# Attention scores with K as the moving operand in two of eight head pairs, and a second exponent in place of a copy of p, in a two-layer decode kernel

## The chip, the core and the metric

The kernel runs on one NeuronCore of a Trainium2 chip. Five engines have their own instruction streams: TensorE (PE in the profile, its weight loads PEld), VectorE (DVE), ScalarE (ACT), GpSimd (POOL) and SyncE (SP), which here only issues DMAs. The time is that of the device for one execution, in microseconds (us); the kernel before was run three times: 1097.86, 1098.34 and 1098.76 us, median 1098.34.

## The reference

Eight sequences (B = 8), one new token each, width D = 448. Two layers run one after the other, each an attention over a cache of 4096 keys followed by a small MLP block; both layers use the same caches and weights.

```python
def _A_ref(x, k_cache, v_cache, wq, wo):
    B, Sq, D = x.shape
    Hq, Dh = 16, 256
    Hkv = k_cache.shape[1]          # 8
    rep = Hq // Hkv                 # 2
    q = (x @ wq).reshape(B, Sq, Hq, Dh).transpose(0, 2, 1, 3)
    k = jnp.repeat(k_cache, rep, axis=1)
    v = jnp.repeat(v_cache, rep, axis=1)
    scores = jnp.einsum("bhqd,bhkd->bhqk", q, k) * (Dh ** -0.5)
    p = _softmax(scores, axis=-1)
    o = jnp.einsum("bhqk,bhkd->bhqd", p, v)
    return o.transpose(0, 2, 1, 3).reshape(B, Sq, Hq * Dh) @ wo
...
x = A_x
x = x + _A_ref(_layernorm(x), A_k_cache, A_v_cache, A_wq, A_wo)
x = x + _B_ref(_layernorm(x), B_w1, B_w2, B_w3, B_w4)
x = x + _A_ref(_layernorm(x), A_k_cache, A_v_cache, A_wq, A_wo)
x = x + _B_ref(_layernorm(x), B_w1, B_w2, B_w3, B_w4)
```

Each of the two caches holds 8 x 8 x 4096 x 256 bf16, 134 MB. Two query heads share one head of K and V.

## The kernel before

**Pieces and slots.** A head's K or V is read as four pieces of 128 partitions x 2048 bf16 (0.52 MB); each piece holds 1024 keys, 8 to a partition. Pieces lie in 31 equal slots of SBUF. Two heads make a pair m, four pairs (m = 0 to 3) a sequence. One DMA brings one, two or four neighbouring pieces (0.5, 1 or 2 MB) into neighbouring slots.

**What runs over what.** For each sequence b the first layer's four pairs are done, then the MLP and the new queries, then the second layer's four pairs, mixed with the first layer's pairs of sequence b + 1. K of pairs 1, 2 and 3 (24 pieces) stays in its slots from the first layer to the second, so only pair 0's K is read twice; V is read in both layers. The stretch from the end of a sequence's first layer to its first scores in the second, about 22 us, is called its turn (`turn`): a chain of small steps on TensorE, VectorE and ScalarE (MLP, query projection), during which the V of the previous sequence's second-layer pairs 2 and 3 streams through the few slots that are left.

**Scores** (`kpart`). K has to be turned so that the key's features lie on partitions. This is done in one of two ways. With `NN` a pair says how many pieces of each head TensorE transposes (line 810, into PSUM; ScalarE copies them back, line 871); these are scored by line 881 (K stationary, two columns of queries). All other pieces are transposed in 32 x 32 blocks by VectorE, half a piece to an instruction (line 893), into another slot, and scored by line 902: for each half piece eight matmuls with a 128 x 128 block of K as the stationary operand and eight columns of queries (`qe`, made by `diagonal`) moving. Scores of a pair stand in one PSUM bank `psS` (two banks) as 128 x 128.

**Softmax of a pair.** Maximum per partition and head (line 916, DVE), over partitions (918, POOL), subtraction (920, DVE), exponent (925, ACT) into the tile `pT`; TensorE transposes that (931), and VectorE moves it to the order that the V of block-transposed pieces needs (939). For the pieces that TensorE transposed no reordering is needed, and POOL copies their part of `pT` into a tile of its own, `pN` (928). Sums and reciprocals: 933, 943, 944.

**p times V** (`vpart`). Usually V moves: four matmuls of 8 x 512 to a piece, in four 32-column groups of the array, one bank `psV` for the pair (line 1005; then 1016, 1018, 1027, 1031). The last pair of a sequence in the first layer is done the other way, V stationary and two columns of p moving, 16 matmuls to a piece (line 977). It is the pair right ahead of the turn.

**At the turn** the second layer's new pieces of pair 3 that TensorE transposes are parked in PSUM until slots are free (`staying`, `park`, `unpark`): one half of them goes into the bank `psS` that the first layer's pair 3 has just used, so this transpose (line 810 into psS) waits for that pair's last reader of the bank.

**Order.** Nothing is ordered on the chip: `Plan.schedule` plays the whole program on the host with a cost for each step, gives each piece its slot, and fixes the order of each engine's instructions; waits are semaphores on the step that is needed. SP's DMA queue is in order too: the loads stand in one fixed sequence, and each waits for the last readers of the slots that it fills. A 2 MB group is split in two if four neighbouring slots are not free when its turn comes.

Of the kernel before, what the change touches and what calls it, by code (L numbers as in the profile page):

```python
# [3 lines left out]
P = 128  # L4
B = 8
D = 448
# [5 lines left out]
NCH = 4  # L12
NSLOT = 31
SLOT = 2048
# [5 lines left out]
NN = ((1, 0, 1, 1), (0, 0, 0, 1))  # L20
NZ = 3
# [65 lines left out]
class Plan:  # L87
# [79 lines left out]
    def schedule(self, order, nslot):  # L167
# [77 lines left out]
        while remaining or nxt[0] < len(order):  # L245
# [58 lines left out]
            for e in ("pe", "dve", "act", "pool"):  # L304
# [9 lines left out]
                if best is None or slot_free[best][0] > t + 1e-6:  # L314
                    cand = [o for o in cand if o.target is None or o.target.slot is not None]
                if not cand:
                    continue
# [38 lines left out]
def bass_interleave_layers__gqa_block_cached__mixer_s_mlp__decode_kernel(  # L356
# [24 lines left out]

    slabs = [sb(f"slot{i}", [P, SLOT * min(4, NSLOT - i)], bf) for i in range(0, NSLOT, 4)]
    slots = [slabs[i // 4][:, SLOT * (i % 4):SLOT * (i % 4 + 1)] for i in range(NSLOT)]
# [11 lines left out]
    pN = sb("pN", [P, 48 * NZ], bf)  # L395

    def pack(name, dt, sizes):
        t = sb(name, [P, sum(sizes)], dt)
        return [t[:, sum(sizes[:i]):sum(sizes[:i + 1])] for i in range(len(sizes))]

    sf, rcs, stat = pack("small32", f32, [8, NP * 4, NS * 8])
    ones, sx1, syn, wgt, quarter, q2, xT, *o1 = pack("small16", bf, [2, 5, 15, 5, 4, 8, 40, 32, 32])
# [3 lines left out]
    sht = qe[:, 164:178]  # L406
    syn = syn.rearrange("p (k c) -> p k c", c=3)
# [29 lines left out]
    def chunks(cache, b, h, name, skip=(), most=2):  # L437
# [4 lines left out]
        def emit(e, u):  # L442
            c, n = int(u.name[-1]), len(u.group)
            return e.dma_start(slabs[u.slot // 4][:, SLOT * (u.slot % 4):SLOT * (u.slot % 4 + n)], src[:, SLOT * c:SLOT * (c + n)])
# [20 lines left out]
    for i, (v0, p0, p1, k0, k1) in enumerate(((1.0, 0, P, 0, 2), (0.0, 0, 64, 1, 2))):  # L465
        add("dve", lambda v, a=(v0, p0, p1, k0, k1): v.memset(ones[a[1]:a[2], a[3]:a[4]], a[0]), 100,
            reads=[Bwgt], writes=[Bwgt], name=f"c4{i}")
# [14 lines left out]

    Bs = {k: Buf() for k in ("x1", "x4", "xy", "xw", "yn", "sq", "f", "f1", "xc", "jk", "hf", "ht")}
    Bx, Bx4 = [Buf() for _ in range(B)], [Buf() for _ in range(B)]
    BpT, BpZ, BpN, Brc = ([Buf() for _ in range(n)] for n in (NP, NP, NZ, NP))
    add("dve", lambda v: v.memset(syn, 0.0), 100, writes=[Bs["yn"]], name="c9")
    add("dve", lambda v: v.memset(pN[:, :], 0.0), 100, writes=BpN, name="cN")
    add("dve", lambda v: v.memset(sx1[64:128, 4:5], 0.0), 100, writes=[Bs["x4"]], name="c5")
# [13 lines left out]
    def total(x, nb, out0, bufs, units, name):  # L502

        def emit(e):
            for c in range(4):
                last = e.matmul(psT[:, out0:out0 + nb], ones[:, c // 3:c // 3 + 1].to_broadcast([P, P]), x(c), start=(c == 0), stop=(c == 3))
# [85 lines left out]
    Bqe, nq = [[Buf(), Bs["hf"]], [Buf()] + [Bs[k] for k in ("xy", "xw", "xc", "jk", "ht")]], [0]  # L592
# [3 lines left out]
    def diagonal(layer, b, m):  # L596
# [29 lines left out]
        dve(put, 210, [Bsel], Bqe[k], [bT], name=n)  # L626
        return k

    def turn(b):

        n = f"turn{b}"
        plan.turn, keep = True, plan.prio
        plan.prio = -1.0
        x = xT[:, :, b]
        dve(lambda e: e.tensor_reduce(sjk[:, :], psT[:, 0:32].rearrange("p (s c) -> p c s", c=4), axis=AX.X, op=ALU.add),
# [38 lines left out]
        dve(lambda e: e.tensor_copy(q2, psT[:, 88:96]), 180, [], [Bq2], [bT], name=n + "q2")  # L674
# [112 lines left out]
    free_p, free_n = list(range(NP)), list(range(NZ))  # L787
# [4 lines left out]
    def apart(t, nn):  # L792

        return t[:, 0:48 * nn].rearrange("p (a c u r) -> p a c r u", a=4, u=3, r=4)[:, :, :, :, 0:3:2]
# [19 lines left out]
    def kpart(at, layer, b, m, kept, most=2):  # L814
# [8 lines left out]
        nn = p.nn = max(nns)  # L823
        n = p.n = f"{'AB'[layer]}{b}m{m}"
# [4 lines left out]
        p.z = z = free_n[len(free_n) - 2:] if nn > 1 else free_n[:nn]  # L829
        for i in z:  # L830
            free_n.remove(i)
# [476 lines left out]
```

## Time and profile before

| what | before |
|---|---|
| runs, median | 1098.34 us |
| the profiled execution | 1099.27 us, its span 1097.5 us |
| bytes moved | 448.96 MB, mean 409 GB/s |
| busy: PE, DVE, ACT, POOL | 760.9, 831.1, 195.0, 79.3 us |
| line 893, transposes of K by VectorE | 544, 648.7 us busy |
| line 902, scores of their halves | 7040 matmuls, 275.7 us busy |
| line 1005, p times V | 1536 + 224 matmuls, 197.9 + 27.4 us busy |

Busy time of an engine is the time in which at least one of its instructions runs. The share of DMA is that of 16 DMA engines having a packet under way; GB/s is what arrived. In a row by stretch each engine's busy time is followed by its number of instructions; then come the granted TensorE clock (1.00 is full), the DMA share and GB/s.

### The profile page before, as it was taken

How to read it: one execution, taken by the hardware profiler on the slowest of the kernel's cores; microseconds unless marked ns; L12 is line 12 of the kernel's file. 1: busy time of each engine (PE TensorE's matmuls, PEld its weight loads, DVE VectorE, ACT ScalarE, POOL GpSimd, SP SyncE). 2: the span in 40 equal slices, each digit the busy share in tenths (PEclk: the TensorE clock that was granted, in tenths of full speed). 3: DMA queues.
4: the chain of work that ended last, by engine and by line, in shares of the span. 5: the costliest groups of instructions: out<-in, count | busy, mean ns of one | idle time of the engine just before them, and what ended most of it. 6: DMA issues, size and time to landing. Idle time of an engine off the chain costs nothing.

```text
span 1097.5 us, 33719 instructions
## 1 busy us (share of the span) xinstructions
PE 760.9 (69%) x15416; PEld 521.1 (47%) x15416; DVE 831.1 (76%) x1556; ACT 195.0 (18%) x281; POOL 79.3 (7%) x256
## 2 busy tenths in 40 slices
PE   2576586768667875768757777578766787577865
PEld 2355454455445543555435554355544455345544
DVE  3999459964996499855999469984799739995472
ACT  1032120212011211212102122121121221121200
POOL 0000001000100010000000000000100001000010
PEclk9995565555555655556555565555555665555555
DMA  9999999999999999999999999999999999999994
GB/s 354 406 420 418 395 406 427 422 411 412 427 422 413 407 428 425 421 397 410 425 428 420 409 415 423 426 420 398 426 425 424 418 394 426 427 422 411 401 426 175
DMA packets 55135, 448.96 MB, mean 409 GB/s; under 512 B 5568, under 2 KB 11600, under 8 KB 14416
## 3 DMA queue, kind: packets, MB, share of 16 engines
q1 hardware_dynamic: 54992, 446.80, 98.4%
q8 instruction: 121, 1.98, 0.7%
q14 instruction: 22, 0.18, 0.0%
HBM read 446.77 MB, written 0.01 MB: 407 GB/s over the span
## 4 chain that ended last, share of the span: by engine, by line
DMA 36%; DVE 32%; PE 21%; issue 7%; ACT 1%; POOL 0%; DVEq 0%; POOLq 0%
DMA slot<-in_A_k_cache_dram 26%; DVE slot L893 23%; DMA slot<-in_A_v_cache_dram 9%; PE psV L1005 7%; PE psS L902 5%; PE psT L656 2%; DVE pT L939 2%; DVE slot L1018 1%; PE psT L587 1%; PE psV L977 1%; PE psS L881 1%; PE psT L1054 1%; DVE qe L623 1%; DVE psS L920 1%; DVE small L916 1%
## 5 line engine op out<-in xcount | busy, mean ns | idle before, releaser
L893 DVE STREAM_TRANSPOSE slot<-slot 128x1024 bf16<-128x1024 bf16 x544 | 648.7, 1228 | 37.6 <-DMA slot<-in_A_k_cache_dram 32.8
L902 PE MATMUL psS<-qe,slot 128*128 128x8 bf16 x7040 | 275.7, 175 | 195.9 <-DVE slot L893 156.8
L902 PEld LDWEIGHTS psS<-qe,slot 128*128 128x128 bf16 x7040 | 232.6, 104 | 332.0 <-DVE slot L893 262.4
L1005 PE MATMUL psV<-slot,pT 128*8 128x512 bf16 x1536 | 197.9, 587 | 7.6 <-DMA slot<-in_A_v_cache_dram 2.6
L871 ACT COPY slot<-psK 128x1024 bf16<-128x1024 bf16 x80 | 78.3, 1015 | 175.7 <-PE psK L810 175.6
L1016 ACT ACTIVATE slot<-psV 128x512 bf16<-128x512 f32 x55 | 33.2, 603 | 344.2 <-PE psV L1005 298.1
L810 PE MATMUL psK<-ident,slot 128*128 128x128 bf16 x640 | 74.6, 308 | 6.6 <-DMA slot<-in_A_k_cache_dram 6.5
L918 POOL PARTITION_ALL_REDUCE small<-small x64 | 23.8, 372 | 692.9 <-DVE small L916 690.9
L810 PEld LDWEIGHTS psK<-ident,slot 128*128 128x128 bf16 x640 | 63.8, 143 | 7.9 <-DMA slot<-in_A_k_cache_dram 7.4
L939 DVE STREAM_TRANSPOSE pT<-psS 128x128 bf16<-128x128 bf16 x64 | 44.9, 702 | 4.3 <-PE psS L931 2.1
L1005 PEld LDWEIGHTS psV<-slot,pT 128*8 128x8 bf16 x1536 | 30.9, 90 | 31.5 <-issue 16.9
L1018 DVE TENSOR_TENSOR slot<-psV,slot 128x512 bf16<-128x512 f32 x55 | 37.1, 675 | 11.5 <-ACT slot L1016 11.5
L925 ACT ACTIVATE pT<-psS 128x128 bf16<-128x128 f32 x64 | 18.0, 281 | 155.4 <-DVE psS L920 155.4
L980 DVE TENSOR_REDUCE small<-psV 128x8 f32<-128x32 f32 x9 | 1.7, 191 | 57.3 <-PE psV L977 57.3
L610 DVE TENSOR_TENSOR qe<-psT,small 128x32 bf16<-128x32 f32 x32 | 6.6, 207 | 48.2 <-PE psS L902 34.3
L1027 PE MATMUL psV<-same,slot 128*128 128x4 bf16 x376 | 16.8, 166 | 31.9 <-DVE slot L1018 31.9
L977 PE MATMUL psV<-pT,slot 128*128 128x2 bf16 x896 | 28.4, 166 | 12.4 <-DMA slot<-in_A_v_cache_dram 11.3
L881 PE MATMUL psS<-qo,slot 128*128 128x2 bf16 x768 | 28.1, 167 | 12.9 <-DVE qo L721 6.4
L881 PEld LDWEIGHTS psS<-qo,slot 128*128 128x128 bf16 x768 | 24.1, 102 | 26.1 <-ACT slot L871 19.6
L1054 PE MATMUL psT<-small,wo_sb 128*128 128x1 bf16 x1024 | 33.4, 165 | 2.2 <-DVE small L1031 1.5
L1054 PEld LDWEIGHTS psT<-small,wo_sb 128*128 128x128 bf16 x1024 | 30.9, 104 | 6.9 <-DVE small L983 3.2
L977 PEld LDWEIGHTS psV<-pT,slot 128*128 128x128 bf16 x896 | 27.0, 105 | 14.2 <-DMA slot<-in_A_v_cache_dram 11.4
(148 smaller groups left out, 668.5 us busy)
## 6 DMA issues: line engine op xcount, KB each, us to landing
slot<-in_A_v_cache_dram SPq DMA_DIRECT2D x148, 1024.0 KB, 9.8
slot<-in_A_v_cache_dram SPq DMA_DIRECT2D x50, 2048.0 KB, 19.4
slot<-in_A_k_cache_dram SPq DMA_DIRECT2D x43, 2048.0 KB, 20.2
slot<-in_A_k_cache_dram SPq DMA_DIRECT2D x73, 1024.0 KB, 14.3
slot<-in_A_v_cache_dram SPq DMA_DIRECT2D x16, 512.0 KB, 6.9
wo_sb<-in_A_wo_dram SPq DMA_DIRECT2D x4, 896.0 KB, 19.5
wq_sb<-in_A_wq_dram SPq DMA_DIRECT2D x3, 1024.0 KB, 9.3
w_sb<-in_B_w_dram SPq DMA_DIRECT2D x1, 1568.0 KB, 21.3
```

The costliest lines, as they stand in the source:

```text
L810: last = e.transpose(tile[:, j * P:(j + 1) * P], slots[u.slot][:, o:o + P], ident[:, :])
L871: return e.copy(slots[u.slot][:, 1024 * t:1024 * t + 1024], tile)
L881: last = e.matmul(o, slots[u.slot][:, i:i + P], q, start=(cc == 0), stop=(cc == 1))
L893: return e.transpose(o, i)
L902: last = e.matmul(o, slots[u.slot][:, i:i + P], qe[:, 128 * k + 64 * s + 8 * g:128 * k + 64 * s + 8 * g + 8], start=(g == 0), stop=(g == 7))
L918: add("pool", lambda g: g.partition_all_reduce(gm, pm, P, ReduceOp.max), 450, [B_["pm"]], [B_["gm"]], prio=pr, name=n + "gm")
L939: add("dve", lambda e: e.transpose(pZ[:, :, 0:3:2].rearrange("p n s r -> p n r s"), psS[x][:, 128:192].bitcast(bf).rearrange("p (n r s) -> ...
L977: last = e.matmul(o, slots[u.slot][:, i:i + P], w, start=(j == 0), stop=(j == 7))
L1005: last = e.matmul(psV[x][32 * i:32 * i + 8, :].rearrange("p (k d) -> p k d", k=2), w, v, start=(s == 0 and c == 0), stop=(s == 1 and c == ...
L1016: add("act", lambda e: e.activation(part(0), psV[x][:, :], ACT.Copy), 590, [], [Bhalf[0]], [bV[x]], [v], prio=at - 1, name=n + "ve0").targ ...
L1018: add("dve", lambda e: e.tensor_tensor(part(1), psV[x][:, :], part(0), ALU.subtract), 590, [Bhalf[0]], [Bhalf[1]], [bV[x]], [v], prio=at - ...
L1054: last = e.matmul(psT[:, 4 * (2 * s + i) + c:4 * (2 * s + i) + c + 1], wo_sb[:, a, d0:d0 + P], o1[b % 2][:, a:a + 1], start=(k == 0), stop ...
```

## The change

1. **Wide scores.** In the first layer's pair 1 and the second layer's pair 0 (`WIDE`; all their pieces are block-transposed), line 902 is replaced by `wide`: eight columns of queries are the stationary operand and K moves, 512 columns (two pieces' blocks at once) to a matmul where the two slots are close enough, 256 otherwise. The two halves of a head's pieces go to two 32-column groups, each head eight steps of two groups. A head's scores begin when all four of its pieces are transposed. The score bank is then 8 rows in four groups x 512.
2. **Softmax of the wide pairs.** The maximum runs over 512 columns, two small DVE steps spread it to heads and back (`m4`, `bi`, with constants `own` and `other`), the exponent runs over 128 x 512 into a free slot, TensorE brings it back to 128 x 128 (`narrow`, eight matmuls), ScalarE copies that into `pT`. The subtraction falls away.
3. **No `pN`.** The POOL copy (line 928) is gone. After the reordering transpose (line 939) ScalarE computes the exponent a second time, from the score bank, for the pieces that TensorE transposed, straight into their places in `pT`. This holds for all pairs with such pieces.
4. **Second layer, pair 2.** Its first piece of each head, which TensorE transposed when it was read in the first layer, is now scored by line 881's form; before it was scored by line 902's. Eight query columns become 16 (`q2`).
5. **Small things.** All slots lie in one tensor; small tiles are packed in one, `syn` and `sx1` move into `qe` and are cleared at each turn (two memsets). Some costs of the planner are changed, and VectorE's transposes may not take the last free slot when an exponent waits for one. The sequence of loads is as before, but slots, waits and splits come from a new plan.

```diff
-NN = ((1, 0, 1, 1), (0, 0, 0, 1))
+NN = ((1, 0, 1, 1), (0, 0, 1, 1))
+WIDE = ((0, 1), (1, 0))
...
+        dve(lambda e: e.memset(syn, 0.0), 125, [], [Bs["yn"]], name=n + "c0")
+        dve(lambda e: e.memset(sx1[64:128, 4:5], 0.0), 125, [], [Bs["x4"]], name=n + "c1")
...
+        def wide(heads, g0, g1):
+            us = [u for s in heads for u in p.K[NCH * s:NCH * s + NCH]]
+
+            def emit(e):
+                for g in range(g0, g1):
+                    for s in heads:
+                        for u in range(2):
+                            (lo, _), (hi, _) = two(s, u)
+                            r = 32 * (2 * s + u)
+                            K = slab.rearrange("p (n t g i) -> p n t g i", t=2, g=8, i=P)
+                            o = psS[x][r:r + 8, :].rearrange("p (n t i) -> p n t i", n=2, t=2)
+                            q = qe[:, 128 * k + 64 * s + 8 * g:128 * k + 64 * s + 8 * g + 8]
+                            if hi - lo < 16:
+                                last = e.matmul(o, q, K[:, lo:hi + 1:hi - lo, :, g, :], start=(g == 0), stop=(g == 7))
+                            else:
...
+        if p.wide:
+            for heads in ([(0, 1)] if kept else [(0,), (1,)]):
+                for g in range(0, 8, 2 if kept else 4):
+                    wide(heads, g, g + (2 if kept else 4))
...
+            add("dve", lambda e: e.tensor_reduce(mx, psS[x][:, :], axis=AX.X, op=ALU.max), 590, [], [B_["mx"]], [bS[x]], prio=pr, name=n + "mx")
+            add("dve", lambda e: e.tensor_scalar(pm, other, mx, None, ALU.add), 70, [Bown, B_["mx"]], [B_["pm"]], prio=pr, name=n + "m4")
...
+            add("dve", lambda e: e.tensor_tensor_reduce(out=pm[:, 0:3].bitcast(bf)[:, 0:5], in0=gm1, in1=own, scale=1.0, scalar=0.0,
+                                                        op0=ALU.mult, op1=ALU.add, accum_out=bias),
+                100, [B_["gm"], Bown], [B_["pm"], B_["mx"]], prio=pr, name=n + "bi")
+            add("act", lambda e: e.activation(pW(), psS[x][:, :], ACT.Exp, bias=bias, scale=INV_SQRT_DH),
+                590, [B_["mx"]], [Bp], [bS[x]], [v], prio=pr, name=n + "ex").target = v
...
+            add("pe", narrow, 300, [Bp, Bc], [], [bS[x]], [v], prio=pr, name=n + "px", n=8)
+            add("act", lambda e: e.copy(pE, xs), 290, [], [BpT[y], BpZ[y]], [bS[x]], prio=pr, name=n + "pe")
...
-        for c in range(nn):
-            add("pool", lambda g, c=c: g.tensor_copy(apart(w, nn)[:, :, c], pE.rearrange("p (a c r s) -> p a c r s", a=4, c=4, r=4)[:, :, c]),
-                200, [BpZ[y]], [BpN[i] for i in z], prio=pr, name=n + f"pn{c}")
...
+        for c in range(nn):
+            ss = slice(sum(c >= w for w in nns), 2)
+            add("act", lambda e, c=c, ss=ss: e.activation(apart(pT[y])[:, :, c, :, ss], xs.rearrange("p (a c r s) -> p a c r s", a=4, c=4, r=4)[:, :, c, :, ss],
+                                                          ACT.Exp, scale=INV_SQRT_DH), 230, [], [BpT[y]], [bS[x]], prio=pr, name=n + f"pn{c}")
```

## The prediction

> **What bounds the kernel now.** I read the page's slices first, then stretches of one sequence, then the groups, then one turn in order of time. On the page:
>
> ```profile
> span 1097.5 us, 33719 instructions
> PE 760.9 (69%) x15416; PEld 521.1 (47%) x15416; DVE 831.1 (76%) x1556; ACT 195.0 (18%) x281; POOL 79.3 (7%) x256
> DMA  9999999999999999999999999999999999999994
> GB/s 354 406 420 418 395 406 427 422 411 412 427 422 413 407 428 425 421 397 410 425 428 420 409 415 423 426 420 398 426 425 424 418 394 426 427 422 411 401 426 175
> q8 instruction: 121, 1.98, 0.7%
> ```
>
> No engine is full, DMA is in every slice but the last. The best slices move 428 GB/s; 448.96 MB at that rate take 1049 us. DMA ends near 1081.5 us, and about 16 us of end chain follow. So some 32 us are lost while DMA runs, and the dips come once a sequence. The stretches of one sequence (the first from a table of 8 us rows, whose sum from 384 to 480 us is the last line):
>
> ```profile
> 432.00:440.00 8.00, 4.18 (x71) 2.20 (x72) 7.50 (x7) 0.08 (x1) 0.00 (x0) 0.50 1.00 424
> 464.00:472.00 8.00, 6.11 (x124) 4.39 (x121) 7.69 (x12) 0.00 (x0) 0.55 (x2) 0.57 1.01 419
> 485.50:491.50 6.00, 4.42 (x132) 3.59 (x129) 0.56 (x4) 0.00 (x0) 0.00 (x0) 0.50 0.96 341
> 491.50:500.50 9.00, 7.54 (x156) 4.32 (x156) 5.25 (x40) 0.21 (x1) 0.79 (x2) 0.50 1.00 419
> 500.50:504.50 4.00, 3.63 (x47) 1.21 (x40) 1.53 (x6) 2.51 (x4) 0.00 (x0) 0.74 0.99 328
> sum 96.00, PE 64.52 PEld 42.99 DVE 87.38 ACT 15.30 POOL 7.35; mean PE 5.38 PEld 3.58 DVE 7.28 ACT 1.28 POOL 0.61
> ```
>
> Outside the turn DMA moves 419 to 432 GB/s, though VectorE is nearly full: many loads are queued, so what the engines do there costs nothing. The turn has two dips: (428 - 341)/428 x 6.0 = 1.22 us and (428 - 328)/428 x 4.0 = 0.93 us, some 2.2 us a sequence, 17 of the 32 us over eight. What the change is worth is decided there. The groups that give the prices:
>
> ```profile
> L893 DVE STREAM_TRANSPOSE slot<-slot 128x1024 bf16<-128x1024 bf16 x544 | 648.7, 1228 | 37.6 <-DMA slot<-in_A_k_cache_dram 32.8
> L902 PE MATMUL psS<-qe,slot 128*128 128x8 bf16 x7040 | 275.7, 175 | 195.9 <-DVE slot L893 156.8
> L1005 PE MATMUL psV<-slot,pT 128*8 128x512 bf16 x1536 | 197.9, 587 | 7.6 <-DMA slot<-in_A_v_cache_dram 2.6
> L1018 DVE TENSOR_TENSOR slot<-psV,slot 128x512 bf16<-128x512 f32 x55 | 37.1, 675 | 11.5 <-ACT slot L1016 11.5
> L916 DVE TENSOR_REDUCE small<-psS 128x4 f32<-128x128 f32 x64 | 17.6, 275 | 13.8 <-PE psS L902 13.8
> ```
>
> And the head of that turn in order of time, TensorE and one step of VectorE:
>
> ```profile
> 482.92 0.56 PE L977 MATMUL psV<-pN,slot 128*128 128x2 bf16 x16
> 483.52 1.03 PE L810 MATMUL psS<-ident,slot 128*128 128x128 bf16 x8
> 484.35 1.47 PE L977 MATMUL psV<-pT,slot 128*128 128x2 bf16 x48
> 487.79 0.24 PE L977 MATMUL psV<-pN,slot 128*128 128x2 bf16 x3 [1.20 <-issue]
> 482.74 0.73 DVE L939 STREAM_TRANSPOSE pT<-psS 128x128 bf16<-128x128 bf16 x1
> ```
>
> The first piece of V is used at 482.92, ahead of VectorE's reordering, because POOL's copy `pN` is ready; later TensorE stands 1.20 us inside the last pair's V. SP issues the V loads of this turn at 482.30 and 483.51 (0.5 MB each), then 1 MB each at 485.85, 488.49, 489.34, 491.80, 495.18, 498.99, 500.88.
>
> **Part by part.**
>
> *Wide scores, TensorE.* Two pairs of each of eight sequences: 16 x 128 = 2048 matmuls of line 902 go, 275.7/7040 = 39 ns each, -80 us. In come 16 x 16 = 256 steps of two column groups. A step of line 1005 with four groups takes 4 x 197.9/1536 = 0.515 us. Two groups in one step are not in the trace: at least half of that, 0.26 (sum 66 us), at most a whole step, 0.515 (132 us). I take the whole, since 512 columns have to pass in either case. `narrow`: 128 matmuls, at most line 810's 74.6/640 = 117 ns, 15 us. TensorE does 14 fewer to 67 us more, by my choice +67 us, 8.4 a sequence. Hidden by the 96 - 64.52 = 31.5 us in which it idles between 384 and 480 us, where both wide pairs lie; without that cover it would cost the 8.4 us.
>
> *Wide softmax, VectorE.* Maximum over 512 columns by line 1018's 0.675 instead of 0.275, two small steps (0.17 and 0.25, by the turn's small steps of that form), less the subtraction's 0.278: +0.54 us a pair, with the two memsets 1.2 us a sequence. Cover: 96 - 87.38 = 8.6 us of idle VectorE. ScalarE: exponent 0.603 and copy 0.281 for 0.281, and six second exponents a sequence of at most 0.28: +2.9 us on an engine that idles 80 of 96.
>
> *Latency of a wide pair.* From its last transpose to p: now about 2.6 us, then 2 x 2.06 (the second head's scores) + 0.675 + 0.17 + 0.37 + 0.25 + 0.60 + 0.94 + 0.28 + 0.28 + 0.70 = 8.4 us. Behind it on the engines' queues VectorE has four transposes, 4.9 us, before it needs the maximum. In the planned order VectorE's transposes of the second head of pair 0 wait for a slot that the first head's wide scores free, with 4 x 1.23 = 4.9 us of transposes between; the scores take 4.1. V waits longer by 5.8 us for p, one or two loads of the 6 to 12 MB then under way (the issued loads less the packets that had ended). No time.
>
> *Second layer, pair 2.* 256 matmuls of 39 ns become 256 of line 881's 28.1/768 = 37 ns: nothing.
>
> *No `pN`.* The one edit at the turn. In the new order the first V piece of the last pair stands behind the parked transpose into `psS`, and that behind the second exponent, which follows line 939. From the rows: 939 ends at 483.47, exponent to about 483.85, transpose (1.03) to about 485.0, so the 0.5 MB load that went at 483.51, and that now waits for this transpose, goes at 485.2: 1.7 us late. The next loads, by the order, wait for one or two V pieces earlier than before, since one more slot is in the round: 1 MB each at about 486.1, 486.9, 488.49, 489.34 (before 485.85, 488.49, 489.34, 491.80). The later ones wait for the same steps of the turn's chain as before: 495.18, 498.99, 500.88. Now the balance. At 479.2 us 2.48 MB were under way, empty at 428 GB/s by 485.0. I let data flow 2.0 us after an issue has ended (0.33 us); that value I choose, as it gives gaps of 0.72 + 0.19 + 0.70 = 1.6 us for before, against 2.2 lost. For after the same sum gives 1.3 us at the first dip and 0.3 at the second: 1.6 again. What the first dip loses the second gives back, because the later loads hang on the chain. Bounds for this part: -1.2 us a turn (first dip filled, second not deepened) to +0.9 (0.54 more at the first dip, nothing back, and 0.4 of later V).
> The turn starts when the last V piece has been used, and TensorE waited 1.20 us for its data; V pieces that come up to 1.05 us later stay inside that.
>
> *Loads.* Five fewer 2 MB loads, in 1 MB instead: 10.5 MB at 419 (the 464 row) and not 427 GB/s: +0.5 us. Instructions: 2563 fewer of 33719 (2640 fewer on TensorE); their own DMA took 0.7% of 1097.5 = 7.7 us: -0.6 us.
>
> The Trainium skill ("DMA: Bandwidth & Descriptors", on measured bandwidth) gives 341 GB/s for a transfer of 1 MB and 425 for 16 MB. That speaks against the splits: 10.5 MB would take 6 us more by it, an estimate from that page, and the sum would be +6. The 464 row, fed by 1 MB loads, shows 419.
>
> *Start.* Some ten small constants and two memsets of 0.48 us on VectorE, before 21 us, when it waits for POOL (8.3 us of idle). Nothing.
>
> Sum: 0 (turns) + 0.5 - 0.6, within 0.2 us of nothing. Against the profiled execution: span 1097.4, and 1.8 us around it (1099.27 - 1097.5). That execution is 0.9 above the median of 1098.34, so I predict 1098.3.
>
> **The rivals.**
>
> *Later turns (slower).* The place is the first V piece behind the second exponent; the price the upper bound, 0.9 us x 8 = 7 us, 1105. For: it delays 0.5 MB just when under 1.5 MB are under way. Against: the earlier 1 MB loads. It decides if V of the last pair ends later than before, that is once the delay exceeds the 1.20 us wait.
>
> *Fuller first dip (faster).* The earlier loads fill the 341 GB/s stretch, and the second dip stays as it is: 1.2 x 8 = 10 us, 1088; half of it 1093. For: three loads go 1.6 to 2.5 us earlier. Against: what is issued by 499 us is the same.
>
> *Column groups that don't overlap (slower).* If each of the two groups takes a whole 0.515, a head's scores take 8.2 us and not 4.1, and VectorE waits 4.1 us four times a sequence, 16 us against 8.6 of slack: 8 x 7.8 = 62 us, 1160; half of it 1129. Against: line 1005 overlaps four.
>
> *Small loads.* A 1 MB load as slow as an isolated one. The nearest rows are the dips, 341 GB/s: 10.5 MB lose 6 us, 1104. Against: the 464 row. It is the skill's rule above.
>
> *It does not do what it says.* TensorE's instructions fall by 9%, its busy time may rise; as it is not the bound, this is the first case.
>
> **How the numbers follow.** No change 0.45, the fuller dip 0.27, later turns 0.19, column groups 0.06, small loads 0.03. A measurement of this kernel tells 0.2%, 2.2 us, from no change. Faster is the fuller dip, 0.27; same 0.45; slower the other three, 0.28. The likeliest case has 1096 to 1101 (half a microsecond a turn is not known to me). To leave out no more than 2 in 10, the range reaches over most of the fuller dip and of later turns: 1090 to 1107.
>
> **What would show it.** Right: the two stretches of a turn hold together the same loss, the first dip deeper or shifted, the second shallower; 424 GB/s and more between turns; line 977's first piece about 1.5 us later; VectorE near 840, TensorE 750 to 830 us busy. Wrong: V of the last pair ending later against its loads, SP waiting on wide scores with less than 1.5 MB under way, VectorE idle behind wide scores, or a step of two groups well above 0.515 us.

## The result and the profile after

The changed kernel took 1103.14 us (median of 12 runs, 1100.80 to 1108.18) and the kernel before, on the same chip, 1098.55 us (12 runs, 1097.31 to 1100.84): ratio 1.0048, 95% interval 1.0032 to 1.0064. Forecast was no change, 1098.3 us; it is 4.6 us slower, and its runs lie further apart than those of before. (Sequences are counted from 0 below, and 0.2% is still what counts as a difference.)

The first profiled execution of the changed kernel is the shortest of its twelve (1100.80 us). Its page, the lines that answer to those shown of before:

```profile
span 1099.0 us, 31149 instructions
PE 751.6 (68%) x14096; PEld 482.7 (44%) x14096; DVE 838.5 (76%) x1609; ACT 222.4 (20%) x345; POOL 67.2 (6%) x216
DMA  9999999999999999999999999999999999999994
GB/s 346 406 420 419 398 404 427 423 395 411 429 423 409 408 426 426 422 389 416 428 427 419 402 418 426 428 418 397 425 426 425 415 392 427 427 423 385 415 427 186
q8 instruction: 110, 1.80, 0.7%
```

Still no engine is full and DMA still runs in every slice; the best slices still move 428 GB/s. The same stretches of sequence 3 as before, those of the turn 1.5 us later since data lags by that much here:

```profile
432.00:440.00 8.00, 4.24 (x32) 1.19 (x32) 7.93 (x8) 0.29 (x1) 0.00 (x0) 0.65 1.00 426
464.00:472.00 8.00, 6.09 (x130) 4.08 (x129) 7.21 (x14) 2.52 (x4) 0.95 (x3) 0.71 1.02 421
487.00:493.00 6.00, 5.62 (x170) 4.71 (x168) 0.73 (x4) 0.00 (x0) 0.00 (x0) 0.50 0.99 347
493.00:502.00 9.00, 7.54 (x160) 4.36 (x160) 5.18 (x39) 0.21 (x1) 0.79 (x2) 0.50 1.01 422
502.00:506.00 4.00, 2.91 (x48) 0.97 (x40) 1.45 (x6) 3.18 (x4) 0.00 (x0) 0.95 0.99 379
```

The first dip is as deep as it was (347 GB/s, before 341), the second shallower (379, before 328): this one turn loses nothing, as the prediction's balance said. The loss is in other turns, and in this shortest execution hardly to be seen. So the kernel was profiled a second time, in an execution of ordinary length (1104.97 us). The groups there:

```profile
L909 DVE STREAM_TRANSPOSE slots<-slots 128x1024 bf16<-128x1024 bf16 x544 | 646.6, 1226 | 40.9 <-PE psS L897 14.5
L1078 PE MATMUL psV<-slots,pT 128*8 128x512 bf16 x1760 | 206.7, 544 | 53.6 <-DMA slots<-in_A_v_cache_dram 39.7
L918 PE MATMUL psS<-qe,slots 128*128 128x8 bf16 x4736 | 172.1, 174 | 78.6 <-DVE slots L909 39.1
L946 PE MATMUL psS<-slots,qe 128*8 128x512 bf16 x424 | 105.6, 573 | 31.6 <-DVE slots L909 31.6
L950 PE MATMUL psS<-slots,qe 128*8 128x256 bf16 x176 | 38.0, 405 | 1.4 <-DVE slots L909 1.4
```

TensorE's idle time ahead of p times V (line 1078) has grown to 53.6 us, most of it ended by a DMA of V; before it was 8.5 us in all (7.6 in the group of line 1005 shown, 0.9 in its group with `pN`). TensorE now stands before data. It does so in the first profile too (55.8 us), so this wait comes with the change in every execution and is not itself the time lost. Where the data fell behind is seen by comparing, byte for byte, when as much had landed as in the kernel before (from the packets' ends, averaged over 8 us; the columns lie between the turns, which fall at 246, 357, 489, 620, 751, 882 and 1014 us):

| us later than before, at | 223 | 259 | 392 | 525 | 657 | 777 | 921 | 1054 |
|---|---|---|---|---|---|---|---|---|
| changed, first profile (1100.80) | 0.4 | 1.5 | 1.3 | 1.3 | 1.5 | 1.3 | 1.7 | 2.3 |
| changed, second profile (1104.97) | 0.7 | 1.7 | 2.1 | 1.5 | 3.5 | 3.1 | 5.0 | 6.4 |

Read every 6 us, the second profile loses nothing lasting between turns; each of its steps of 1 to 2 us stands at a turn (at 246, 620, 882 and 1014 us). Now the turn of sequence 4, the stretches 617 to 627 us, first before, then the second profile of the changed kernel:

```profile
617.00:622.00 5.00, 3.58 (x107) 2.95 (x105) 0.36 (x2) 0.00 (x0) 0.00 (x0) 0.50 0.99 383
622.00:627.00 5.00, 3.82 (x90) 2.33 (x87) 3.52 (x28) 0.20 (x1) 0.40 (x1) 0.50 1.02 419
```
```profile
617.00:622.00 5.00, 4.46 (x125) 4.23 (x126) 1.35 (x5) 0.59 (x2) 0.55 (x2) 0.50 0.84 291
622.00:627.00 5.00, 4.02 (x109) 2.97 (x107) 1.59 (x10) 0.00 (x0) 0.00 (x0) 0.50 1.00 384
```

The DMA engines, busy at 0.99 before, stand at 0.84: there was too little to load. At 620 us 0.29 MB were under way (issued loads less ended packets), before 2.03. What differs is first seen 25 to 40 us earlier, in SP's issues of loads, before:

```profile
570.85 0.33 SPq L444 DMA_DIRECT2D slot<-in_A_v_cache_dram  x1
574.73 0.33 SPq L444 DMA_DIRECT2D slot<-in_A_k_cache_dram  x1
581.57 0.33 SPq L444 DMA_DIRECT2D slot<-in_A_v_cache_dram  x1
582.42 0.33 SPq L444 DMA_DIRECT2D slot<-in_A_k_cache_dram  x1
590.04 0.33 SPq L444 DMA_DIRECT2D slot<-in_A_v_cache_dram  x1
```

and changed, second profile:

```profile
572.31 0.33 SPq L450 DMA_DIRECT2D slots<-in_A_v_cache_dram  x1
577.71 0.33 SPq L450 DMA_DIRECT2D slots<-in_A_k_cache_dram  x1
592.51 0.33 SPq L450 DMA_DIRECT2D slots<-in_A_v_cache_dram  x1
595.05 0.33 SPq L450 DMA_DIRECT2D slots<-in_A_k_cache_dram  x1
595.76 0.33 SPq L450 DMA_DIRECT2D slots<-in_A_v_cache_dram  x1
```

Before, the longest gap in these rows is 7.6 us (the longest of this sequence, 10.3 us, stands ahead of them, from 552.65 on); now nothing goes for 14.8 us. The load at 592.51 (V of pair 2) fills slots in which pieces 0 and 1 of pair 1's V lie, and these are used when pair 1's p is there. SP's queue is in order, so the K loads behind it wait too. 14.8 us at 420 GB/s are 6.2 MB: under way were 7.4 MB at 576 us and 1.8 at 594, before 7.7 and 3.3.

The hole itself closes again: at 617 us 0.92 MB are under way, before 1.01. What is still late by then is work. The last pair's K, which landed 0.8 to 1.2 us later than before, is transposed some 4 us later by TensorE (606.00 us, before 601.83) and by VectorE (610.72, before 606.77); its V is first used 5.8 us later (619.94, before 614.18), and the two loads just ahead of the dip go 4.0 and 5.4 us later (617.57 and 620.17, before 613.55 and 614.77). Which single wait hands the hole on to this work was not followed.

Nor does the hole always cost time. Ahead of each of the five turns from 489 us on SP stands for 14.3 to 15.1 us in both profiles, while these ten turns, each taken from 22 us before it to 20 us after, lie between a gain of 0.8 us and a loss of 1.8. The four that lose 0.8 us or more are those in which less than 0.35 MB were under way at the lowest; in the others it was never below 0.43. What makes one execution come closer to empty than another is open.

And why p is late: VectorE between the last transpose of pair 1's K and the reordering of its p in sequence 4, before,

```profile
573.43 1.23 DVE L893 STREAM_TRANSPOSE slot<-slot 128x1024 bf16<-128x1024 bf16 x1
...
575.78 0.25 DVE L916 TENSOR_REDUCE small<-psS 128x4 f32<-128x128 f32 x1
...
577.11 0.27 DVE L920 TENSOR_TENSOR psS<-psS,small 128x128 f32<-128x128 f32 x1
...
578.79 0.71 DVE L939 STREAM_TRANSPOSE pT<-psS 128x128 bf16<-128x128 bf16 x1
```

and changed, second profile, followed by the wide scores of the pair's second head on TensorE:

```profile
576.46 1.23 DVE L909 STREAM_TRANSPOSE slots<-slots 128x1024 bf16<-128x1024 bf16 x1
...
577.65 6.04 DVE L909 STREAM_TRANSPOSE slots<-slots 128x1024 bf16<-128x1024 bf16 x5
583.61 0.65 DVE L975 TENSOR_REDUCE small<-psS 128x1 f32<-128x512 f32 x1
584.19 1.23 DVE L909 STREAM_TRANSPOSE slots<-slots 128x1024 bf16<-128x1024 bf16 x1
585.34 0.19 DVE L976 TENSOR_SCALAR small<-small 128x4 f32<-128x4 bf16 x1
...
586.09 0.17 DVE L983 CUSTOM_DVE_ANT_0 small<-small 128x5 bf16<-128x5 f32 x1 [0.25 <-POOL small L980]
...
588.92 1.23 DVE L909 STREAM_TRANSPOSE slots<-slots 128x1024 bf16<-128x1024 bf16 x1
590.08 0.68 DVE L1011 STREAM_TRANSPOSE pT<-psS 128x128 bf16<-128x128 bf16 x1
```
```profile
577.83 3.06 PE L946 MATMUL psS<-slots,qe 128*8 128x512 bf16 x16
```

From the end of the transpose (574.66; 577.69) to the end of the reordering (579.50; 590.76): 4.8 us before, 13.1 after. Only 3.2 us of the 8.2 more are the wide scores (577.69 to the end of TensorE's 577.83 + 3.06 = 580.89); the maximum then waits another 2.7 us behind transposes of the next pair that stand ahead of it in VectorE's order, and more transposes stand between the steps that follow.

### The profile page after: what moved, and what is told of

Read it like the earlier page. It is cut to its first block, busy times and chain, and to the rows that moved or that the text cites. A ratio compares the mean times of both kernels' runs of the same rounds, so it can differ in the third digit from the quotient of the medians.

```text
span 1099.0 us, 31149 instructions
## 1 busy us (share of the span) xinstructions
PE 751.6 (68%) x14096; PEld 482.7 (44%) x14096; DVE 838.5 (76%) x1609; ACT 222.4 (20%) x345; POOL 67.2 (6%) x216
## 4 chain that ended last, share of the span: by engine, by line
DVE 42%; PE 27%; DMA 15%; issue 9%; SPq 4%; ACT 2%; POOL 0%; DVEq 0%; POOLq 0%; ACTq 0%
DVE slots L909 31%; DMA slots<-in_A_k_cache_dram 9%; PE psV L1078 8%; DMA slots<-in_A_v_cache_dram 6%; PE psS L918 6%; SPq L431 3%; DVE pT L1011 3%; PE psS L897 2%; PE psV L1052 2%; DVE slots L1091 2%; PE psT L674 1%; PE psT L603 1%; ACT slots L887 1%; PE psK L828 1%; PE psT L1125 1%
## 5 line engine op out<-in xcount | busy, mean ns | idle before, releaser
L909 DVE STREAM_TRANSPOSE slots<-slots 128x1024 bf16<-128x1024 bf16 x544 | 647.1, 1227 | 43.2 <-PE psS L897 15.1
L1078 PE MATMUL psV<-slots,pT 128*8 128x512 bf16 x1760 | 208.9, 547 | 55.8 <-DMA slots<-in_A_v_cache_dram 41.8
L918 PE MATMUL psS<-qe,slots 128*128 128x8 bf16 x4736 | 171.8, 174 | 78.7 <-DVE slots L909 39.5
L918 PEld LDWEIGHTS psS<-qe,slots 128*128 128x128 bf16 x4736 | 150.9, 103 | 142.7 <-DVE slots L909 78.0
L946 PE MATMUL psS<-slots,qe 128*8 128x512 bf16 x424 | 106.6, 582 | 27.9 <-DVE slots L909 27.8
L887 ACT COPY slots<-psK 128x1024 bf16<-128x1024 bf16 x80 | 79.1, 1013 | 144.2 <-PE psK L828 144.1
L1078 PEld LDWEIGHTS psV<-slots,pT 128*8 128x8 bf16 x1760 | 38.1, 90 | 103.1 <-issue 52.8
L828 PE MATMUL psK<-ident,slots 128*128 128x128 bf16 x640 | 71.5, 287 | 8.9 <-DMA slots<-in_A_k_cache_dram 8.9
L828 PEld LDWEIGHTS psK<-ident,slots 128*128 128x128 bf16 x640 | 56.8, 131 | 18.8 <-DMA slots<-in_A_k_cache_dram 10.6
L1100 PE MATMUL psV<-same,slots 128*128 128x4 bf16 x376 | 16.5, 166 | 62.2 <-DVE slots L1091 58.9
L1091 DVE TENSOR_TENSOR slots<-psV,slots 128x512 bf16<-128x512 f32 x55 | 37.1, 675 | 9.5 <-ACT slots L1089 9.1
```

The source lines that it names most:

```text
L828: last = e.transpose(tile[:, j * P:(j + 1) * P], slots[u.slot][:, o:o + P], ident[:, :])
L887: return e.copy(slots[u.slot][:, 1024 * t:1024 * t + 1024], tile)
L909: return e.transpose(o, i)
L918: last = e.matmul(o, slots[u.slot][:, i:i + P], qe[:, 128 * k + 64 * s + 8 * g:128 * k + 64 * s + 8 * g + 8], start=(g == 0), stop=(g == 7))
L946: last = e.matmul(o, q, K[:, lo:hi + 1:hi - lo, :, g, :], start=(g == 0), stop=(g == 7))
L1078: last = e.matmul(psV[x][32 * i:32 * i + 8, :].rearrange("p (k d) -> p k d", k=2), w, v, start=(s == 0 and c == 0), stop=(s == 1 and c == ...
```

## The experiments

All times are against runs of the kernel before on the same chip; in brackets the 95% interval of the ratio.

**Which part.** Three theories. *Wide*: the first layer's pair 1 has its p late, and loads ahead of the turn with it. *Second exponent*: the first piece of V at the turn is late (the prediction's slower rival). *Plan*: a new order costs or wins some microseconds by luck.

The change again:

> The changed kernel as it stands, once more, to have a second profile and five more rounds of it. Every theory expects the ratio seen already, 1.003 to 1.006 of the kernel before (1102 to 1105 us). What it is to show is where a run of ordinary length loses the 3 us that the first profiled execution (1100.8 us, the shortest of twelve) had not lost: by 'wide' behind the first layer's pair 1, in the stretch from its maximum to the turn; by 'second exponent' between the last pair's p and its V inside the turn.

1.0049 [1.0036, 1.0062], 1104.83 us; its profile is the second one above.

```diff
-WIDE = ((0, 1), (1, 0))
+WIDE = ()
```

> The changed kernel with no pair scored wide (the list of wide pairs is empty); pN stays away, the second exponent and the second layer's pair 2 stay as in the change. Theory 'wide': the long way to the first layer's pair 1's p was what it cost, so about 1098.5 us, ratio 0.999 to 1.002; maximum to last reordering of that pair back from some 6.5 us to below 4 us. Theory 'second exponent': the late first piece of V at the turn was what it cost, so it stays at 1102 to 1105, ratio 1.003 to 1.006. Theory 'plan': any new order costs or wins some microseconds; this run then lies anywhere from 1095 to 1106 and its sum with the run that has the wide scores alone does not come to +4.6 us.

1.0014 [1.0005, 1.0023], 1100.88 us.

```diff
-NN = ((1, 0, 1, 1), (0, 0, 1, 1))
+NN = ((1, 0, 1, 1), (0, 0, 0, 1))
+NZ = 3
...
+        for c in range(nn):
+            add("pool", lambda g, c=c: g.tensor_copy(apart(w, nn)[:, :, c], pE.rearrange("p (a c r s) -> p a c r s", a=4, c=4, r=4)[:, :, c]),
+                200, [BpZ[y]], [BpN[i] for i in z], prio=pr, name=n + f"pn{c}")
...
-            add("act", lambda e, c=c, ss=ss: e.activation(apart(pT[y])[:, :, c, :, ss], xs.rearrange("p (a c r s) -> p a c r s", a=4, c=4, r=4)[:, :, c, :, ss],
-                                                          ACT.Exp, scale=INV_SQRT_DH), 230, [], [BpT[y]], [bS[x]], prio=pr, name=n + f"pn{c}")
...
```

> The changed kernel with POOL's copies pN back (three places) and the second layer's pair 2 scored as before, so the kernel before with two wide pairs a sequence and the small tables. Theory 'wide': 1102 to 1105 us, ratio 1.003 to 1.006, with the first layer's pair 1's p as late as in the change. Theory 'second exponent': about 1098.5 us, ratio 0.999 to 1.002. Theory 'plan': anywhere from 1095 to 1106.

1.0049 [1.0036, 1.0061], 1104.19 us.

```diff
-                        E = add("dve", square, 1135, [], [], [], [u.source, u], prio=pr + 0.005 * t, name=f"{n}D{s}{c}{t}")
+                        E = add("dve", square, 1155, [], [], [], [u.source, u], prio=pr + 0.005 * t, name=f"{n}D{s}{c}{t}")
...
-        dve(put, 210, [Bsel], Bqe[k], [bT], name=n)
+        dve(put, 270, [Bsel], Bqe[k], [bT], name=n)
...
-            220, [], [BpT[y]], [bS[x]], prio=pr, name=n + "pq")
+            430, [], [BpT[y]], [bS[x]], prio=pr, name=n + "pq")
```

> The kernel before with nothing changed but three durations that its planner assumes (a transpose of K 1155 for 1135, spreading q 270 for 210, reordering p 430 for 220), which the change alters as well; the instructions are the same, their order may move. Theories 'wide' and 'second exponent': 1097.5 to 1099.5 us, ratio 0.999 to 1.001. Theory 'plan': a ratio off by 0.002 or more, to either side, from the order alone.

0.9996 [0.9987, 1.0005], 1098.47 us. These three numbers of the planner do nothing; that another order could cost some microseconds is not excluded by that alone. The wide scores alone bring the whole loss and without them 0.0014 is left: *wide*, and a small rest outside it.

**Which wide pair, and is it the late p?** In each of the next two one pair is taken off the list.

```diff
-WIDE = ((0, 1), (1, 0))
+WIDE = ((0, 1),)
```

> The changed kernel with one wide pair only, the first layer's pair 1, whose p is needed by the last V loads ahead of the turn. The version with no wide pair stood at ratio 1.0014, the whole change at 1.0049. Theory 'late p ahead of the turn': nearly all of the 0.0035 between them is here, ratio 1.004 to 1.0055. Theory 'wide work of either pair': half of it, 1.003. Theory 'second layer': 1.001 to 1.002.

1.0059 [1.0044, 1.0074], 1106.83 us.

```diff
-WIDE = ((0, 1), (1, 0))
+WIDE = ((1, 0),)
```

> The changed kernel with one wide pair only, the second layer's pair 0, whose scores follow the turn. Theory 'late p ahead of the turn': as with no wide pair, ratio 1.0005 to 1.0023. Theory 'wide work of either pair': 1.003. Theory 'second layer': 1.004 to 1.0055.

0.9997 [0.9988, 1.0005], 1099.11 us. The second layer's pair costs nothing, the first layer's all of it. The next puts the delay into the kernel before, with no wide scores and no work on a busy engine:

```diff
-        add("pool", lambda g: g.partition_all_reduce(gm, pm, P, ReduceOp.max), 450, [B_["pm"]], [B_["gm"]], prio=pr, name=n + "gm")
+        for i in range(19 if (layer, m) == (0, 1) else 1):
+            add("pool", lambda g: g.partition_all_reduce(gm, pm, P, ReduceOp.max), 450, [B_["pm"]], [B_["gm"]], prio=pr, name=n + "gm" + "x" * (18 - i) * ((layer, m) == (0, 1)))
```

> The kernel before, with the maximum over the partitions of the first layer's pair 1 taken nineteen times over on POOL instead of once; the result is the same, p comes some 18 x 0.46 = 8.3 us later (4.85 to about 13 us after the pair's last transpose, as in the change), and nothing is added on TensorE, VectorE, ScalarE or in the transfers; K goes free as early as before. Theory 'late p ahead of the turn': ratio 1.003 to 1.005 by the delay alone. Rival 'K held': the wide scores let go of K only at their end, and it is that which costs; then the delay alone gives 0.999 to 1.001. Rival 'engine work': TensorE's and VectorE's added work is what costs; then 0.999 to 1.001 too.

1.0036 [1.0023, 1.0050], 1103.78 us; from sequence 1 on p is ready 13.6 to 14.1 us after the last transpose. SP's issues around the same place:

```profile
577.38 0.33 SPq L444 DMA_DIRECT2D slot<-in_A_k_cache_dram  x1
593.83 0.33 SPq L444 DMA_DIRECT2D slot<-in_A_v_cache_dram  x1
```

The same hole, 16.5 us. Here too it stands ahead of every turn (15.9 to 16.5 us), and the turn of sequence 4 loses nothing in this execution (1101.31 us; table below). So a late p of this pair is enough for a loss of that size: 0.0036 here against 0.0045 for the wide pair (1.0059 less 1.0014), and the intervals overlap. Whether the wide pair has a second, smaller cost beside it was tested further down.

The last of this group, for the small rest:

```diff
-NN = ((1, 0, 1, 1), (0, 0, 1, 1))
-WIDE = ((0, 1), (1, 0))
+NN = ((1, 0, 1, 1), (0, 0, 0, 1))
+WIDE = ()
```

> The changed kernel with no wide pair and with the second layer's pair 2 scored as before: what is left is the second exponent in place of POOL's copies, and the small tables. With pair 2 as in the change it stood at 1.0014 (1.0005 to 1.0023). Theory 'second exponent': the same 1.0005 to 1.0025, by the late first piece of V at the turn. Rival 'pair 2': 0.999 to 1.0005.

1.0005 [0.9989, 1.0020], 1099.78 us. Inconclusive: it overlaps with both answers. That the second exponent costs up to 2 us is not excluded; that it costs the 4.6 is.

**Place and dose.** The wide pair moved from the first layer's pair 1 to its pair 0, whose V waits for other reasons after p:

```diff
-WIDE = ((0, 1), (1, 0))
+WIDE = ((0, 0), (1, 0))
```

> The changed kernel with its first-layer wide pair moved from pair 1 to pair 0; as many wide scores and wide maxima as in the change. In the kernel before, V of pair 0 is first used 5.5 us after p (555.45 to 561.00 us in the fourth sequence), that of pair 1 0.8 us after p. Theory 'late p ahead of the turn': most of the loss goes, ratio 1.000 to 1.002. Rival 'engine work': 1.0045 or more, as in the change.

1.0064 [1.0051, 1.0077], 1105.46 us: my theory's number was wrong. The comparison byte for byte (table below) shows that 4.2 us are lost before the first turn, and in the trace between 89 and 101 us: sequence 1's pair 0 is scored while sequence 0 is still running, and a load of K that in the kernel before went at 86.04 us (its second half at 87.82) waits for its wide scores until 92.17, with 0.2 MB under way at 90 us and nothing at 92. SP's wait:

```profile
SPq L450 <- PE psS L950: 5.9, 1, 5.9
```

The seven turns that the table shows cost 1.2 us together, about what they cost with no wide pair (0.6). A late release ahead of a thin place again, but of K and at another place; a run below tests this reading.

```diff
-        for i in range(19 if (layer, m) == (0, 1) else 1):
+        for i in range(19 if (layer, m) == (0, 0) else 1):
```

> The kernel before with the nineteenfold maximum on POOL at the first layer's pair 0 and not at pair 1: the same work, the same 8.3 us on p. Theory 'late p ahead of the turn': 5.5 of the 8.3 us are waited for anyway, so ratio 0.999 to 1.0015. Rival 'any late p': as with the delay at pair 1, 1.0036.

1.0005 [0.9996, 1.0015], 1099.25 us: the same delay does no harm at this place. It is not that nobody waits: the longest gap in SP's issues ahead of the turn is 13.8 us in sequence 4 (554.69 to 568.53), before 10.3 at that place. But 10.0 MB were under way when it began and 6.3 when it ended; with the delay at pair 1 the gap took 8.2 MB down to 1.2.

```diff
-        for i in range(19 if (layer, m) == (0, 1) else 1):
+        for i in range(10 if (layer, m) == (0, 1) else 1):
```

> The kernel before with ten maxima in place of nineteen at the first layer's pair 1: p later by 9 x 0.46 = 4.1 us. If the loss grows with the delay: ratio 1.0018. If there is a reserve that has to be used up first: 0.999 to 1.001.

1.0008 [0.9998, 1.0018], 1099.56 us.

```diff
-        for i in range(19 if (layer, m) == (0, 1) else 1):
+        for i in range(37 if (layer, m) == (0, 1) else 1):
```

> The same with thirty-seven maxima: p later by 36 x 0.46 = 16.6 us. If the loss grows with the delay: ratio 1.0072 or more; if the 8.3 us had already emptied what was queued, each further microsecond costs a whole one in eight turns: 1.0036 + 8.3 x 8 / 1099 = 1.06. If the loss had another cause that the reordering brought by chance: 1.002 to 1.005.

1.0394 [1.0374, 1.0413], 1142.76 us. Its slices and the wait of SP that is new:

```profile
GB/s 354 407 403 419 395 413 422 354 386 418 427 378 368 405 426 426 346 378 407 425 429 346 396 409 425 425 334 398 427 426 422 326 402 427 426 382 359 388 427 184
```
```profile
SPq L444 <- DVE psS L921: 141.7, 8, 20.7
```

Delays of about 4, 9 and 17 us cost 0.9 us (not clear of noise), 4.0 and 43 us. In sequence 4 p was ready 4.8, 9.2, 14.1 and 21.7 us after the last transpose (before and the three doses), and the last V piece of the pair was used 16.6, 16.9, 19.0 and 25.9 us after it: up to some 10 us the pair's later V pieces were waiting for their own data anyway, so only the early pieces' slots come free late; beyond that everything behind moves, and SP stands for 17.7 us in each of eight sequences (141.7/8). The loss is no straight line: a reserve is used up first.

**K held, engine work.** First the moved pair, with sequence 1's pair 0 scored narrow:

```diff
-        p.wide = (layer, m) in WIDE
+        p.wide = (layer, m) in WIDE and (layer, b, m) != (0, 1, 0)
```

> The changed kernel with the first layer's wide pair moved to pair 0, as before, but the second sequence's pair 0 scored narrow (one of sixteen wide pairs less). In the trace of the moved version 4.8 of its 5.3 us fall between 89 and 101 us, where a load of K waits for that pair's wide scores (issued at 91.93, in the kernel before at 85.80) and 0.18 MB are under way; the eight turns together lose about what they lose with no wide pair. Theory 'late release ahead of a thin place': ratio 1.000 to 1.0025. Rival 'engine work': 1.005 or more still.

1.0013 [1.0003, 1.0023], 1100.44 us: by one of sixteen wide pairs it is 0.0051 less, 5.6 us, and the reading holds.

Then the kernel before, with the scores of pair 1 held back:

```diff
+        if (layer, m) == (0, 1):
+            for i, S in enumerate(p.scores):
+                for u in p.K[NCH * (i // 8):NCH * (i // 8) + NCH]:
+                    for E in u.evs:
+                        S.deps[E] = True
```

> The kernel before with the narrow scores of the first layer's pair 1 held back until all transposes of their head have ended, as the wide scores must; same instructions, same result, K goes free up to some 8 us later, p some 2 us later. If K held long is a cause by itself in this place: ratio 1.0015 or more. If V waiting for p is all there is: no more than the half delay (4.1 us) had, 1.0000 to 1.0010.

0.9991 [0.9983, 1.0000], 1098.23 us, with this pair's first scores at 564.9 us in sequence 4 instead of 556.9, and p 8.2 us after the last transpose (3.4 later). Holding K costs nothing in this place.

And both wide pairs in the second layer:

```diff
-WIDE = ((0, 1), (1, 0))
+WIDE = ((1, 0), (1, 2))
```

> The changed kernel with both wide pairs in the second layer (pairs 0 and 2, and none in the first): as many wide pairs as in the change. Theory 'late release ahead of the turn': nothing is late ahead of the turn, ratio 0.999 to 1.002, as with pair 0 of the second layer alone (0.9997). Rival 'engine work': 1.0035 or more.

0.9982 [0.9969, 0.9994], 1097.12 us. As many wide pairs as the change, and not slower than before but a little faster; TensorE's idle time ahead of line 1078 is 13.2 us, and the hole in SP's issues is gone:

```profile
574.11 0.33 SPq L450 DMA_DIRECT2D slots<-in_A_k_cache_dram  x1
582.31 0.33 SPq L450 DMA_DIRECT2D slots<-in_A_v_cache_dram  x1
```

The table of bytes, for the runs that tell most (the profiled execution of each, so 1 to 3 us from its median):

| us later than before, at | 223 | 259 | 392 | 525 | 657 | 777 | 921 | 1054 |
|---|---|---|---|---|---|---|---|---|
| no wide pair | 0.5 | 1.9 | 2.6 | 1.8 | 2.0 | 1.9 | 1.9 | 1.1 |
| first layer's pair 1 wide | -0.2 | 2.0 | 4.6 | 5.0 | 6.9 | 6.7 | 7.8 | 7.2 |
| second layer's pair 0 wide | 0.0 | 1.1 | 2.2 | 0.9 | 1.3 | 1.6 | 1.1 | 0.3 |
| moved to the first layer's pair 0 | 4.2 | 6.5 | 7.8 | 6.9 | 6.4 | 7.0 | 6.1 | 5.4 |
| first layer's pair 1 delayed, 19 maxima | 0.7 | 1.1 | 2.7 | 2.7 | 2.8 | 3.3 | 3.0 | 2.3 |
| both in the second layer | 0.2 | 0.0 | 0.4 | -0.6 | -0.9 | -0.9 | -1.2 | -1.9 |

**A version that beats both?** The last one again, and two neighbours.

> The version with both wide pairs in the second layer once more, on whatever chip it falls: ratio 0.997 to 0.9995 if it is faster than the kernel before, 0.9995 to 1.0005 if the first result was luck.

0.9985 [0.9977, 0.9994], 1097.17 us: the gain of 1.4 us repeats, though at 0.15% it is below the 0.2% that this kernel's measurement is trusted with. Against the changed kernel (1104.83 us on the chip where that was run again) it is some 7 us. With the scores of the first layer's pair 1 held back by the same five lines as above:

> The same with the scores of the first layer's pair 1 held back to the end of each head as well, which had given 0.9991 by itself. If the two gains are of different kinds: 0.997 to 0.998. If both are the luck of an order: 0.998 to 1.001.

0.9988 [0.9979, 0.9998], 1097.63 us: nothing more. With POOL's copies back, the version of the wide scores alone with another list:

```diff
-WIDE = ((0, 1), (1, 0))
+WIDE = ((1, 0), (1, 2))
```

> Both wide pairs in the second layer, with POOL's copies back; pair 2 is scored in TensorE's own transposed form in fewer pieces, as in the kernel before. If the second exponent costs something (1.0005 to 1.0014 by the runs without wide pairs): 0.9965 to 0.998. If not: as the version without the copies, 0.998 to 0.999.

0.9991 [0.9981, 1.0001], 1097.75 us: not to be told apart. Why the second layer's wide pairs win over narrow ones (1.0014 with none) was not settled.

## Why the prediction was wrong

*Latency of a wide pair.* This is the step that failed: "V waits longer by 5.8 us for p, one or two loads of the 6 to 12 MB then under way (the issued loads less the packets that had ended). No time." The size was 8.2 us, not 5.8, since both of its terms are bare sums of durations: 2.6 us for before, which measured 4.8, and 8.4 us for after, which measured 13.1. The scores of the second head took 3.2 us, not 4.1, but the transposes that the step itself put "behind it" (four; in the trace five, 6.0 us) stand ahead of the maximum in VectorE's order and had to be added, and others between the small steps too. The weight was worse: it counted the loads that wait and not the queue behind them. No load goes for 14.8 us, 6.2 MB of the 7 to 8 MB under way, and that 28 to 42 us ahead of the turn, which needs the rest. The delay alone, with everything else of the kernel before, gives 1.0036; half of it 1.0008. "No time" would have been nearly right for 4 us and was wrong for 8. The Trainium skill ("TensorE: Matmul & The Clock Gate", the opening table) calls VectorE's queue a strict first-in, first-out one; the maximum that starts at 583.61, 2.7 us after its last score, agrees.

*Wide scores on TensorE.* The cover held: with both wide pairs in the second layer nothing is lost. In size, the scores' groups went from 275.7 us to 172.1 + 105.6 + 38.0 = 315.7, +40. The prediction's terms for them give +42: 132 - 80, less 10 us for the 256 matmuls of the second layer's pair 2 that leave the same group at 39 ns. The choice of a whole step for two column groups was right: 105.6 + 38.0 us over 256 steps are 0.56 us a step, against 0.515 chosen. TensorE's busy time as a whole still fell by 9.3 us and not the +67 that was chosen; it counts overlapping matmuls once, and TensorE's mean granted clock was 0.63, before 0.58. How much the overlap and the clock account for was not worked out.

*Wide softmax.* VectorE +7.4 us (predicted 9.6), ScalarE +27.4 (23): hidden, by the same run.

*No `pN`, the balance at the turn.* At the turn of sequence 3 it came as worked out: first dip as deep, second shallower. The later loads go at the times worked out plus 1.3 us of lag (489.77, 490.68, 496.52, 500.34 and 502.23 us), the three ahead of them another 0.6 to 0.7 us later (487.23, 488.06, 488.92). There the first V piece is used at 486.99 us, not 482.92: 4.1 us later, more than the predicted 1.5 plus 1.3 of lag (the prediction's own rows, with the parked transpose ending at 485.0, already make it about 2). And TensorE's wait of 1.20 us inside that V is gone:

```profile
486.17 1.04 PE L828 MATMUL psS<-ident,slots 128*128 128x128 bf16 x8 [0.35 <-ACT pT L1018]
486.99 3.66 PE L1052 MATMUL psV<-pT,slots 128*128 128x2 bf16 x128
```

The last piece comes 1.34 us later than before, no more than all the data there. Alone, the parts without wide scores cost 0.5 to 1.5 us (1.0005 and 1.0014); the term was zero, and how much of this is real is open.

*Loads.* The stretch from 464 us, whose data come in 1 MB loads in both kernels, moves 421 GB/s (before 419; outside the turn 418 and not 419 was the lowest of the rows from 384 to 480 us), not the 341 that the Trainium skill ("DMA: Bandwidth & Descriptors", measured bandwidth) has for a transfer of 1 MB issued from GpSimd. Five 2 MB loads fewer, as predicted, and small loads as a rival fall.

*The rivals.* *Later turns* had the right sign, the right place of the loss and nearly the time (1105); that is luck, since its price stood for another road. With the second exponent and no wide pair 0.0014 is lost, with wide pairs and no second exponent 0.0049. Of the prediction's signs of being wrong, V of the last pair ending later against its loads is seen only weakly: in sequence 4 of the second profile its last piece ends 3.0 us later than before, and the load of it landed 2.5 us later. *Fuller first dip* did not come; its "three loads go 1.6 to 2.5 us earlier" was misread, since by the prediction's own times one of the three goes only 0.85 us earlier. *Column groups that don't overlap*: two groups took 3.06/8 = 0.38 us a step here, so they overlap.

## What to carry to other kernels

An engine with idle time hides work, not delay: for each step whose result frees buffers, ask which load waits for those buffers, what stands behind that load in an ordered queue, and whether the gap times the bandwidth leaves enough of what is under way for the next thin place. (The same delay cost nothing where 10 MB were under way.) Put a longer chain where its result is not needed at once (here the second layer, 7 us better than ahead of the turn). The cost of a delay has a reserve in front of it, so measure two or three doses before calling one free.

## What the runs showed of the hardware

At the same granted clock a step of two 32-column groups with 512 moving columns each takes as long as a step of four such groups. At a clock of 0.50 eight steps of two took 3.58 us and, in the kernel before, six steps of four (line 1005) 2.73 us, 0.45 and 0.46 us a step:

```profile
963.61 3.58 PE L946 MATMUL psS<-slots,qe 128*8 128x512 bf16 x16 [4.59 <-DVE slots L909]
```
```profile
1065.35 2.73 PE L1005 MATMUL psV<-slot,pT 128*8 128x512 bf16 x24
```

At full clock eight steps of two took 1.89 us (at 316.30 us), and the 3.06 us above fell at a clock of 0.61.

The delayed kernels' times spread more: 1100.33 to 1106.76 us for the delay of 8 us and 1100.80 to 1108.18 for the change, against 1097.31 to 1100.84; that a queue near empty passes small disturbances on is a guess that was not tested.
